# A fused convolution and gated MLP: one stream per row lane and bank, and a shorter fill

## Chip, cores, metric

One core of a Trainium2 chip. The metric is the device time of the program in microseconds (us), median of several runs. In profile lines PE is TensorE, PEld its weight loads, DVE VectorE, ACT ScalarE, POOL GpSimd, SPq and ACTq the queues on which SyncE and ScalarE issue transfers; L208 is line 208 of the kernel.

## Reference

```
x: (8, 4096, 192) f32; weight: (8, 7); w_in: (192, 2048); w_out: (2048, 192)
w   = softmax(weight, axis=-1)               # 8 heads of 24 channels, 7 taps
y   = causal convolution of x over tokens, w[head] for the head's 24 channels
h   = y.reshape(32768, 192) @ w_in
out = (h * cos(h)) @ w_out                   # f32
```

## The kernel before

Tokens run as two streams (batches 0 to 3 and 4 to 7), 512 tokens of each at a time: 32 such tiles, each with 16 *ups* and two *sets* of 16 *downs*, 64 sets in all.

- An **up** (U) makes 128 columns of `h` for both streams: six 64x512 matmuls in two row lanes of 64 rows. ScalarE then takes the cosine (S), VectorE multiplies (M).
- A **down** (d) adds two of these blocks into the output: eight 64x192 matmuls, again in two lanes. The lanes write different PSUM banks, and the program lets them trade banks only after a *mark*: a one-element memset on GpSimd that waits for the one lane's last matmul and is waited for by the next.
- A **convolution** (C and c, its halves) is done on TensorE with band matrices. Here the two lanes are the two halves of one 128-row window, so they add into the same banks and have to trade them once, with a mark:

```
def conv_first():
    ...
    end = lanes(half(0, 0, False), half(1, 1, False))
    return both, ps, (half(1, 0, True), half(0, 1, True)), end
...
elif op == "C":
    state["open"] = conv_first()
    state["mark"] = changeover(state["open"][3])
elif op == "c":
    conv_second(state["open"][2], state.pop("mark"))
```

- A convolved block is copied out of PSUM and transposed by a DMA (e). x is loaded in units, cast to bf16 by GpSimd (p), and loaded ahead.

```
nc.sync.dma_start(out=xw[:, s, :, :], in_=dram(x, base, [[D, 128], [W * D, NB], [1, D]]))   # 128 x 4 x 768 B
```

- The **fill** (k: the next weight load or cast) ends with the 16th up; then one order of operations is repeated for each set. Only what is emitted earlier on an engine or queue runs earlier there.

```
fill("kkkkUkSkMUSMUSMkUSMUSMCUScMekkkUSMkkUSMUSMCUScMekkkUSMkUSMkkkkUSMCUScMekkkkUSMUSMkU")
while count["y"] < 2 * NI:
    emit("dddSMdUdMSdUdMSdUMdSUdSMdUdSMCdcpdeMUdSdUyxUMS")
```

## Time and profile before

| | before |
|---|---|
| median of the 3 runs before the change was timed (range) | 741.77 us (741.24 to 743.03) |
| span of the profiled run | 739.7 us |
| first down | 46.87 us in the chain (46.70 in the timeline) |
| set with / without convolution | 11.02 / 10.46 us |
| end of the 62nd set to the end | 16.5 us |

Three stretches, to be read one by one: the start up to the first down, 62 sets bound by TensorE (50 with a convolution), and a tail. The prediction below shows the lines. Two more of the page will matter, from its parts on the DMA queues (packets, MB, share of 16 engines) and on the DMA issues (count, KB each, median us from issue to landing):

```profile
q1 hardware_dynamic: 126930, 69.88, 37.8%
...
xw<-in_x_dram SPq DMA_DIRECT2D x64, 384.0 KB, 5.4
```

This queue, with all loads of x and nearly all other traffic, stores too, keeps the DMA engines busy 37.8% of the span, and a 384 KB load of x lands 5.4 us after its issue (the median of 64).

### The profile page before, as it was taken

What the parts mean: (1) busy time and instruction counts of PE and PEld (TensorE: products, weight loads), DVE (VectorE), ACT (ScalarE), POOL (GpSimd) and SP (SyncE); (2) the same over time, 40 slices, a digit from 0 to 9 for tenths busy, and PEclk for the clock granted to TensorE, in tenths of its full rate; (3) what the DMA queues carried; (4) which work ended last, traced back from release to release, by engine and by line L of the source; (5) the groups of instructions that cost most, each with busy time, mean ns of one, the idle gap of its engine ahead of it and who ended that gap; (6) DMA issues with size and microseconds to landing.
All of it is one profiled execution on the core that took longest, in us unless ns stands there. A gap on an engine that the chain in (4) does not pass through costs nothing.

```text
span 739.7 us, 26852 instructions
## 1 busy us (share of the span) xinstructions
PE 707.4 (96%) x12044; PEld 518.1 (70%) x12044; DVE 644.3 (87%) x586; ACT 591.1 (80%) x642; POOL 86.1 (12%) x256
## 2 busy tenths in 40 slices
PE   1589999999999999999999999999999999999997
PEld 1257777777777777777777777777777777777776
DVE  1588998998989989989899899899899899999992
ACT  3588888888888888888888888888888887877871
POOL 2340110110110110110110110110111100000000
PEclk9999999999999999999999999999999999999999
DMA  8983453515344354342614615445332210111012
GB/s 188 290 207 70 107 125 77 137 50 155 70 121 112 68 128 116 105 122 70 156 39 110 160 43 144 98 104 140 74 95 61 70 53 25 44 45 44 24 45 66
DMA packets 127879, 73.17 MB, mean 99 GB/s; under 512 B 53907, under 2 KB 126099, under 8 KB 127764
## 3 DMA queue, kind: packets, MB, share of 16 engines
q1 hardware_dynamic: 126930, 69.88, 37.8%
q10 hardware_dynamic: 834, 1.57, 0.9%
q8 instruction: 94, 1.54, 0.9%
q14 instruction: 21, 0.17, 0.1%
HBM read 33.69 MB, written 25.17 MB: 80 GB/s over the span
## 4 chain that ended last, share of the span: by engine, by line
PE 93%; DVE 2%; DMA 2%; ACT 1%; issue 1%; SPq 0%; ACTq 0%; POOLq 0%; POOL 0%; DVEq 0%
PE h L208 48%; PE acc L208 45%; DVE g L332 2%; DMA cT<-ct 1%; ACT cos L327 1%; DMA row_d<-taps 1%; DMA turned<-row_d 0%; SPq L305 0%; ACT ct L297 0%; ACT L131 0%; PE h L404 0%; ACT osb L366 0%; DVE osb L366 0%; ACTq L78 0%; DVE band L159 0%
## 5 line engine op out<-in xcount | busy, mean ns | idle before, releaser
L332 DVE TENSOR_TENSOR g<-h,cos 128x1024 bf16<-128x1024 f32 x512 | 609.9, 1221 | 38.5 <-ACT cos L327 26.6
L327 ACT ACTIVATE cos<-h 128x1024 bf16<-128x1024 f32 x512 | 514.0, 1023 | 115.5 <-PE h L208 98.0
L208 PE MATMUL acc<-w,g 64*128 64x192 bf16 x8192 | 428.2, 243 | 1.3 <-ACT osb L366 0.8
L208 PEld LDWEIGHTS <-g 64*128 64x128 bf16 x8192 | 353.4, 94 | 101.8 <-POOL mark L218 1.4
L208 PE MATMUL h<-cT,w 64*128 64x512 bf16 x3072 | 408.8, 378 | 13.0 <-DMA cT<-ct 7.8
L208 PEld LDWEIGHTS <-w 64*128 64x128 bf16 x3072 | 148.7, 94 | 91.1 <-issue 18.5
L218 POOL MEMSET mark<- 1x1 f32 x117 | 10.3, 88 | 624.6 <-PE acc L208 447.9
L366 DVE COPY osb<-acc 128x384 f32<-128x384 f32 x64 | 35.7, 558 | 38.5 <-PE acc L208 38.4
L119 POOL CAST xb<-xw 128x512 bf16<-128x512 f32 x102 | 59.9, 616 | 6.5 <-DMA xw<-in_x_dram 5.3
L297 ACT CAST ct<-h 112x1024 bf16<-112x1024 f32 x51 | 51.6, 1012 | 10.5 <-PE h L208 9.0
L208 PE MATMUL h<-xb,band 64*128 64x192 bf16 (+5 forms) x760 | 41.7, 223 | 1.9 <-DVE g L332 1.9
L366 ACT COPY osb<-acc 128x384 f32<-128x384 f32 x64 | 30.3, 473 | 11.1 <-PE acc L208 11.1
L208 PEld LDWEIGHTS <-band 64*128 64x128 bf16 x760 | 25.8, 94 | 12.3 <-POOL mark L218 8.3
L404 PE MATMUL h<-xb,band 128*128 128x192 bf16 (+2 forms) x20 | 2.7, 330 | 12.0 <-DVE band L159 12.0
L404 PEld LDWEIGHTS <-band 128*128 128x128 bf16 x20 | 2.3, 143 | 12.1 <-DVE band L159 12.0
L175 POOL CAST w<-xw 128x512 bf16<-128x512 f32 x10 | 6.1, 641 | 9.7 <-DMA xw<-in_moe_w_in_dram 9.7
L159 DVE COPY band<-turned 128x512 bf16<-128x512 bf16 x1 | 0.3, 295 | 7.8 <-DMA turned<-row_d 7.8
L152 ACT CAST xb<-xw 128x768 bf16<-128x768 f32 x2 | 1.7, 831 | 4.0 <-DMA xw<-in_x_dram 4.0
L185 POOL CAST w<-xw 128x384 bf16<-128x384 f32 x8 | 3.7, 512 | 0.0
L175 DVE CAST w<-xw 128x512 bf16<-128x512 f32 x2 | 1.2, 630 | 2.4 <-DMA xw<-in_moe_w_in_dram 2.4
L294 ACT CAST ct<-h 112x512 bf16<-112x512 f32 x4 | 2.3, 585 | 0.9 <-PE h L208 0.9
L297 DVE CAST ct<-h 112x1024 bf16<-112x1024 f32 x1 | 1.2, 1224 | 2.0 <-PE h L404 2.0
(21 smaller groups left out, 15.2 us busy)
## 6 DMA issues: line engine op xcount, KB each, us to landing
xw<-in_x_dram SPq DMA_DIRECT2D x64, 384.0 KB, 5.4
out_dram<-osb SPq DMA_DIRECT2D x64, 384.0 KB, 3.2
xw<-in_x_dram SPq DMA_DIRECT2D x8, 336.0 KB, 4.9
xw<-in_moe_w_in_dram SPq DMA_DIRECT2D x4, 384.0 KB, 5.9
xw<-in_moe_w_in_dram ACTq DMA_DIRECT2D x4, 384.0 KB, 7.1
xw<-in_moe_w_out_dram SPq DMA_DIRECT2D x2, 768.0 KB, 12.1
cT<-ct SPq DMA_TRANSPOSE x67, 3.0
xw<-in_x_dram SPq DMA_DIRECT2D x8, 60.0 KB, 1.8
```

The source lines that it names most:

```text
L119: nc.gpsimd.tensor_copy(out=xb[:, :, :, ch], in_=xw[:, :, :, ch])
L152: copy(out=xb[:, s, :, :], in_=xw[:, s, :, :])
L175: copy(out=w1[:, q, c * CW:(c + 1) * CW], in_=staged[1, c][:, q, :])
L185: nc.gpsimd.tensor_copy(out=w2[:, c * n:(c + 1) * n, :][:, fs, :], in_=staged[2, c][:, fs, :])
L208: ins = nc.tensor.matmul(out=o, lhsT=w, rhs=r, start=start, stop=stop, skip_group_check=True)
L218: ins = nc.gpsimd.memset(mark, 0.0)
L294: nc.scalar.copy(ct[0:W, 0, :], ps[0:W, 0, :])
L297: copy(out=ct[0:W], in_=ps[0:W])
L327: nc.scalar.activation(out=cos, in_=hs[n], func=AF.Sin, bias=math.pi / 2.0, scale=1.0)
L332: nc.vector.tensor_tensor(out=g, in0=hs.pop(n), in1=cs.pop(n), op=ALU.mult)
L366: copy(out=osbs[k][:, 2 * bank:2 * bank + 2, :].rearrange("p a d -> p (a d)"), in_=acc[bank][:, 0:2 * D])
L404: nc.tensor.matmul(out=o, lhsT=band[:, h, :], rhs=r, start=True, stop=True)
```

## The change

Its intent: (1) a convolution on 64-row windows of 56 tokens, so that a lane is a *stream* and has a bank for itself, and no mark is needed; (2) downs in an order that works on the first 8 of 16 blocks longer, with three changes of bank in a set in place of one, so that the fill needs 13 ups in place of 16; (3) the first convolved blocks transposed by the idle array in place of DMA transposes, with 80 idle matmuls to keep its clock up, and loads spread on two queues; (4) the last set in an `h` tile of its own, woven between the downs of the set before, its store split on two queues.

```diff
-    W = 112
+    V = 56
+    BEFORE = L - V
+    W = 2 * V
... lane = (slice(0, L), slice(L, 128)): stream s uses partitions 64 s to 64 s + 63
-                nc.sync.dma_start(out=xw[:, s, :, :], in_=dram(x, base, [[D, 128], [W * D, NB], [1, D]]))
+            queue.dma_start(out=xw[lane[s], w0:w1, :], in_=dram(x, base + w0 * V * D, [[D, L], [V * D, w1 - w0], [1, D]]))
... convolution: lane l reads and writes stream l only
-        end = lanes(half(0, 0, False), half(1, 1, False))
+        mms = [conv_mms(p, ps, l) for l in range(2)]
+        half = len(mms[0]) // 2
+        lanes(*[m[:half] for m in mms])
... loads
-        nc.sync.dma_start(out=st, in_=moe_w_out[...])
+        nc.scalar.dma_start(out=st, in_=moe_w_out[...])
-    load_w1(0)
+    load_w1(0, (nc.scalar, nc.scalar))
     load_w1(1)                       # lower half on SyncE's queue, upper half on ScalarE's
+    load_ahead(1, (nc.sync, nc.scalar))
... turns of the downs
+    TURNS = ((0, 0), (0, 1), (1, 0), (1, 1), (1, 2), (0, 2), (0, 3), (1, 3))
-        if j == 7:
-            state["turn"] = changeover(end)
+        if j < 15 and TURNS[(j + 1) // 2][0] != flip:
+            turns[k] = changeover(end)
... start
+    for _ in range(80):
+        nc.tensor.matmul(out=idle[0:W, 0, 0:W], lhsT=one, rhs=one, start=True, stop=True)
+    ... two convolutions, 15 transposes as matmuls against an identity, four copies
-    fill("kkkkUkSkMUSMUSMkUSMUSMCUScMekkkUSMkkUSMUSMCUScMekkkUSMkUSMkkkkUSMCUScMekkkkUSMUSMkU")
-    while count["y"] < 2 * NI:
-        emit("dddSMdUdMSdUdMSdUMdSUdSMdUdSMCdcpdeMUdSdUyxUMS")
+    fill("kkkkUSMkUSMkUSMkkkkUSMkUSMCcUSMekkCcUSMekkkUSMCcUSMekkkkkkkkUSMUSMUSMkU")
+    for k in range(NSETS - 2):
+        emit("dddSMdUdMSUdSdMUdSMdU" + ("CcpdMSeU" if k == 1 else "dMSU") + "dSdMCcdedMUdpSdUyxUMS")
+    last = h_pool.tile([128, 2, T], FP32, name="h")
+    emit("dddMSdUdMSUdSdMUdSMdMM" + "tttt" + "dddddtttttt" + "ddxytttttt" + "xy")      # t: downs of the last set
```

## The prediction

> **What bounds the kernel now.** I read the busy times first, then the chain of work that ended last in three windows, then the list of waits, then the moved bytes in stretches of 2 us.
>
> ```profile
> PE 707.4 (96%) x12044; PEld 518.1 (70%) x12044; DVE 644.3 (87%) x586; ACT 591.1 (80%) x642; POOL 86.1 (12%) x256
> ...
> PE   1589999999999999999999999999999999999997
> ...
> PE 93%; DVE 2%; DMA 2%; ACT 1%; issue 1%; SPq 0%; ACTq 0%; POOLq 0%; POOL 0%; DVEq 0%
> ```
>
> TensorE is the bound from the third of the 40 slices to the last, and the chain is 93% TensorE. So there are three separate places to gain: the start, the middle, the tail. The start, from the chain between 0 and 60 us:
>
> ```profile
> 3.84 4.35 DMA row_d<-taps
> 8.27 3.34 DMA turned<-row_d
> ...
> 17.05 6.50 DMA cT<-ct
> ...
> 23.59 3.18 PE h L208 x14
> ...
> 46.87 1.32 PE acc L208 x32
> ```
>
> Columns are start, length, what. Two DMA round trips build the band matrices, three transposing DMAs turn the first convolved blocks, the first up-projection ("up") really starts at 23.59, the first output product ("down") at 46.87. Between the last two TensorE is fed by VectorE and ScalarE one tile at a time. The middle, the same view between 300 and 312 us, at the convolution:
>
> ```profile
> 306.74 0.65 PE h L208 x6
> 307.39 0.33 PE acc L208 x8
> 307.72 0.22 PE h L208 x8
> 307.94 0.33 PE acc L208 x8
> 308.27 0.34 PE h L208 x8
> 308.61 0.33 PE acc L208 x8
> ```
>
> An up is 0.65 us, a down 0.33. The convolution's two halves have equal columns, yet the second takes 0.34 and the first 0.22: it waits for the one-element GpSimd mark that tells that the lanes may change banks. A set (8 ups, 16 downs) takes 11.02 us with a convolution and 10.46 without (starts of successive long downs in the chain, 46.87 to 57.89 and 598.14 to 608.60). The waits give the matching line:
>
> ```profile
> PEld L208 <- POOL mark L218: 9.7, 53, 0.5
> ```
>
> 53 waits, one for each convolution; the 64 down marks leave no such stall but in the tail, since an up lies between the two turns: down, up, down at 304.45 to 305.43 is as quick there as elsewhere. The tail, in the chain:
>
> ```profile
> 722.67 0.48 ACT osb L366
> 723.15 0.04 issue
> 723.20 2.83 PE acc L208 x64
> ...
> 732.80 2.86 PE acc L208 x64
> 735.66 0.55 DVE osb L366
> ```
>
> The last two sets have only downs left, done one set after the other, with two bare marks and a bare emptying of the banks between: 723.20 to 735.66 = 12.46 us for 32 downs (32 x 0.328 = 10.5), then the copy and the store to 739.7.
>
> **What the Trainium skill says.** (1) "TensorEngine Tiling (Array Packing)", Gotcha 1: different row tiles must not use one PSUM bank at once. That is why the lanes need marks, and why a bank for each lane needs none. (2) "TensorE: Matmul & The Clock Gate", Wait — 56ns, not 53.3ns?: a warm matmul costs N/2.4 + about 2.5 ns. The trace agrees: 128 of 192 columns and 48 of 512 in two lanes are 10.24 us plus 88 x 2.5 ns = 10.46, the measured set. So the middle has nothing more to give but the convolution. (3) The same page, What's actually happening: the array runs at half clock until some 3.4 us of activity. The trace agrees: the 20 matmuls of the first ups took 4.09 us at 23.59, later six took 0.65 us. (4) "DMA: Bandwidth & Descriptors", Anatomy of one DMA: about 2 us are fixed in each transfer. Here even the 0.2 KB load of the taps landed 1.24 us after issue, and the 2.2 KB row took 4.35 us behind 1.57 MB of x, so most of the latter is queueing.
>
> **The change, part by part.**
>
> *Convolution.* Each lane takes one stream and one bank; two 64-row windows of 56 tokens replace one 128-row window in two halves. Matmuls per usual tile (12 or 16) and columns (1024 per lane) stay. The mark goes. New cost: 1024/2.4 GHz = 0.427, plus 6 to 8 per lane x 2.5 ns = 0.445 us, against 0.555. The loop has 62 sets: before 62 x 10.46 + 50 x 0.555 = 676.3 (measured, 46.87 to 723.20: 676.3); after, 51 of the 56 convolutions fall into it (2 + 3 come earlier): 62 x 10.46 + 51 x 0.445 = **671.2 us, -5.1**. Loads, casts (616 ns), evacuations (1012 ns) and transposes keep their size.
>
> *Turns of the output product.* Three changes of bank in a set in place of one, 192 down marks for 64. In the order of operations each has an up of 0.65 us between; a mark's way is about 0.35 us (0.27 idle in the tail plus the drain), so I count 0. The order lets the first downs use the first 8 f tiles, so the fill needs 13 ups in place of 16. Marks can be late only behind GpSimd casts (2 x 0.62 us), which are placed over 2 us before the next one.
>
> *Start.* Taps ready at 3.8 as before. The row goes on the other queue and behind 0.98 MB of x, which at the 239 to 267 GB/s of the first 8 us has landed by some 6.2: row at 6.1 (estimate). Two half-size turned loads issue to 6.8 and land at about 9.5 beside the w1 loads, band copy 0.3: **convolution at 9.9**, against 11.99. The 80 idle matmuls of 112 columns start at about 2.6 and end by 9 to 10 (31 cold ones of 107 ns, the rest 56 to 80), so the clock is up. Two tiles 0.9 us, evacuation 1.0 to 1.2, transposes by the array 15 x 0.06 to 0.1, four copies in pairs of 0.6 each, handovers: about 3.8 us, so **first up at 13.7**, against 23.59. Before, the fill from first up to first down was 23.3 us = 16 x 1.22 (the multiply, 1221 ns) + 3 convolutions x 1.27. For 13 ups: 15.9 + 3.8 = 19.7, plus 0.6 for two more DMA issues on ScalarE's queue: 20.3. **First down at 34.0.** But the marks of the first set stand behind all weight and x casts on GpSimd. They need 8.8 MB; at 250 GB/s for x alone and 320 (seen 28 to 36 us) for the mix, with three transposes, this has landed at 33 to 34, and the last casts end at 35 to 37, where the first turn wants its mark at 36. I charge 1.2 us: **loop starts, in effect, at 35.2**.
>
> *Tail.* Three ups are left as well, and the last set, in its own h tile, is woven between the downs of the one before: 32 x 0.328 + 3 x 0.65 = 12.5, two bare marks 0.5, copy and drain 0.7, store in two halves on two queues 2.8: **16.5 us**, against 16.5 before without the three ups. So this part earns 2 us, spent on the shorter fill.
>
> *Sum.* 35.2 + 671.2 + 16.5 = 722.9 us span, against 739.7: -16.8. The timed runs are 2.1 us above the span: **725.0 us**, a gain of 2.3%. The same by causes: 11.7 earlier at the loop, of which 3 ups and a convolution (2.5) are done later; 5.1 from the convolution; 2.5 back from the tail.
>
> **Rivals.**
> 1. *The transfers decide the start.* The fill is 10 us earlier but needs nearly the same bytes. For: before, the DMA share was above 1 from 12 to 38 us, and the x load for the last cast of the fill landed at 44.8. Against: three transposes of 6.5 us are gone from it, and the up fill itself is slower than the loads. If loads run at 250 GB/s throughout, the first turn waits to about 40: 729 us, within 2%.
> 2. *The added marks cost after all.* 128 more; at 0.05 us each, 6.4 us, and the gain of the convolution is gone: 731 us. Against: the 64 old ones cost nothing measurable.
> 3. *VectorE becomes the bound.* It works 8 x 1.221 + 0.558 = 10.33 us a set; a set without convolution has 10.46, one with it now 10.91. With three h tiles I find 0.1 to 0.3 us slack at each up; if those are used up in the 51 convolution sets at 0.1 us each, 730 us. For it: the multiplies now come later in the order; against: 10.33 is still below 10.46.
> 4. *The start is better than I think*: turned at 8, fill not held back: 31 to 32, 721 us.
>
> **Range and chances.** The middle is sure to about 1.5 us, start to 3, tail to 1. Low is rival 4 with luck, high is rival 1 plus a part of 2: 719.5 to 731. The 2% border is 726.9, only 1.9 us above my time, so chances follow from that: faster 0.66, same 0.33, slower 0.01.
>
> **What would show it.** In the changed profile: the convolution at 9 to 11, first up at 13 to 15 and first down at 32 to 36; a mid-run convolution set of 10.9 us with no waits for marks in it, and 10.46 without; the list of waits without TensorE waiting for marks beyond some 2 us in all; from the end of the 62nd set 16 to 17 us. Wrong would be: first turn of the first set later than 38 with GpSimd waiting for x or w loads (rival 1), sets of 11 us with TensorE waiting for marks (2) or for the multiply (3), or a band that comes after 11.

## The result

738.4 us (737.64 to 740.11, 4 runs) against 741.62 (4 runs) before: a ratio of **0.9956** with a 95% interval of 0.9934 to 0.9979, so the same within 2%, and outside the predicted range. Ratios here are the mean time of one kernel's runs over that of the other's runs of the same rounds, so not quite the ratio of the medians quoted. The unaltered changed kernel was run again later: 738.62 us, 0.9948.

The span fell from 739.7 to 738.3 us (the profiled run was the slowest of its four). The page of the changed kernel:

```profile
PE 712.4 (96%) x12271; PEld 565.9 (77%) x12271; DVE 640.4 (87%) x590; ACT 588.8 (80%) x637; POOL 94.0 (13%) x340
...
PEclk7689999999999999999999999999999999999999
...
q1 hardware_dynamic: 121712, 66.42, 42.7%
...
PE 93%; DMA 4%; issue 1%; DVE 1%; ACT 1%; POOL 1%; ACTq 0%; SPq 0%; POOLq 0%; DVEq 0%
...
xw<-in_x_dram SPq DMA_DIRECT2D x60, 384.0 KB, 8.0
```

The chain has 4% of DMA where it had 2%. The queue moves *less* (66.42 for 69.88 MB; 3 MB of weights went to the other queue) and is busy *longer* (42.7 for 37.8%); a load of x lands after 8.0 us, not 5.4. The array's granted clock is below full in the first slices.

**The middle is as predicted.** The chain between 309 and 321 us (start, length, what), a set with a convolution:

```profile
309.65 1.32 PE acc L254 x32
...
316.83 0.46 PE h L254 x10
...
320.55 0.49 PE acc L254 x12
```

The convolution is one piece of 0.46 us (0.445 predicted) with no wait for a mark, and the set takes 320.55 - 309.65 = 10.90 us (10.905 predicted). The list of waits between 55 and 720 us:

```profile
PEld L254 <- POOL mark L264: 0.8, 2, 0.4
```

Two waits of 0.4 us for about 190 marks (before, in the same window: 50 waits, 8.6 us). So the added marks cost 0.8 us at most there.

**The start is not.** The chain between 0 and 60 us:

```profile
3.85 4.02 DMA row_d<-taps
...
8.48 7.76 DMA turned<-row_d
...
20.82 2.76 PE h L254 x12
...
23.67 16.43 DMA xw<-in_moe_w_out_dram
...
40.15 1.86 POOL w L219 x4
...
47.01 1.11 POOL xb L156 x2
48.12 0.04 POOL mark L264
```

The band's data ("turned") takes 7.76 us, 16.24 us instead of 9.5; the first up runs at 20.82, not 13.7. Then the chain is a load: w2 on its way for 16.4 us, its casts, the cast of x behind it, and then the mark for the first turn. GpSimd's operations between 8 and 56 us (start, length, what, and in brackets the idle time before with its cause) show what came late before that:

```profile
29.19 0.61 POOL L156 CAST xb<-xw 128x512 bf16<-128x512 f32 x1 [8.25 <-DMA xw<-in_x_dram]
32.03 1.73 POOL L209 CAST w<-xw 128x512 bf16<-128x512 f32 x3 [2.23 <-DMA xw<-in_moe_w_in_dram]
```

The second half of blocks 5 to 12 landed at 29.2 us, and the first convolution of the fill waited for it (3.10 us). The second waited 3.81 us more, but not for x: its casts stood on GpSimd behind the cast of w1, whose load came at 32.0. The first down came at 45.88 us, 0.8 us earlier than before (46.70 in the same view), where 34 was predicted. The DMA engines were busy all the time: the first 35 us moved, by the busy times in stretches of 5 us, (111 + 218 + 205 + 198 + 207 + 278 + 227) x 5 us = 7.2 MB, against 8.2 MB in the kernel before. Two of those stretches, each with the busy time of five engines, the granted clock, the DMA share and GB/s:

```profile
15.00:20.00 5.00, 3.04 (x79) 2.56 (x80) 1.60 (x3) 1.20 (x2) 1.73 (x3) 0.50 1.12 198
20.00:25.00 5.00, 4.85 (x29) 2.31 (x29) 2.50 (x4) 3.06 (x5) 0.61 (x1) 0.55 1.11 207
```

A full DMA share (1.12; a packet is counted where it starts, so a share can pass 1) at 198 GB/s; in the kernel before the stretches at a full share between 10 and 45 us had 206 to 328 GB/s.

**The tail** is 1.3 us longer than predicted. The operations between 726 and 740 us:

```profile
727.63 1.49 PE L254 MATMUL acc<-w,g 64*128 64x192 bf16 x32 [0.58 <-POOL mark L264]
...
734.23 0.48 ACT L398 COPY osb<-h 128x384 f32<-128x384 f32 x1 [1.92 <-PE h L254]
...
734.74 0.56 DVE L398 COPY osb<-h 128x384 f32<-128x384 f32 x1 [2.39 <-ACT osb L398]
```

The two bare marks took 0.58 and 0.27 us, 0.85 together where 0.5 was predicted, and the two last copies ran one after the other (VectorE names ScalarE's copy as its releaser). From the last long run of downs of the loop (720.49) to the end it took 17.8 us, three ups included.

### The profile page after: what moved, and what is told of

The parts are those of the page before. It is cut to its first block, busy times and chain, and to the rows that moved or that the text cites. A ratio compares the mean times of both kernels' runs of the same rounds, so it can differ in the third digit from the quotient of the medians.

```text
span 738.3 us, 27466 instructions
## 1 busy us (share of the span) xinstructions
PE 712.4 (96%) x12271; PEld 565.9 (77%) x12271; DVE 640.4 (87%) x590; ACT 588.8 (80%) x637; POOL 94.0 (13%) x340
## 3 DMA queue, kind: packets, MB, share of 16 engines
q1 hardware_dynamic: 121712, 66.42, 42.7%
## 4 chain that ended last, share of the span: by engine, by line
PE 93%; DMA 4%; issue 1%; DVE 1%; ACT 1%; POOL 1%; ACTq 0%; SPq 0%; POOLq 0%; DVEq 0%
PE h L254 48%; PE acc L254 45%; DMA xw<-in_moe_w_out_dram 2%; DMA turned<-row_d 1%; DMA row_d<-taps 1%; DVE g L361 0%; POOL w L219 0%; ACT L170 0%; POOL xb L156 0%; ACT cos L356 0%; ACT ct L309 0%; PE acc L456 0%; DVE osb L398 0%; ACTq L79 0%; ACT cT L459 0%
## 5 line engine op out<-in xcount | busy, mean ns | idle before, releaser
L254 PEld LDWEIGHTS <-g 64*128 64x128 bf16 x8192 | 374.8, 94 | 84.2 <-POOL mark L264 2.8
L254 PE MATMUL h<-cT,w 64*128 64x512 bf16 x3072 | 423.7, 380 | 1.7 <-DVE g L361 1.6
L254 PEld LDWEIGHTS <-w 64*128 64x128 bf16 x3072 | 179.0, 95 | 63.2 <-issue 7.8
L264 POOL MEMSET mark<- 1x1 f32 x192 | 16.9, 88 | 608.1 <-PE acc L254 599.5
L309 ACT CAST ct<-h 112x1024 bf16<-112x1024 f32 (+1 forms) x55 | 55.3, 1006 | 14.6 <-PE h L254 10.7
L156 POOL CAST xb<-xw 128x512 bf16<-128x512 f32 (+1 forms) x110 | 64.4, 615 | 14.9 <-DMA xw<-in_x_dram 14.0
L254 PE MATMUL h<-xb,band 64*128 64x192 bf16 (+8 forms) x912 | 38.0, 218 | 15.6 <-DVE band L237 7.8
L254 PEld LDWEIGHTS <-band 64*128 64x128 bf16 x912 | 32.8, 96 | 17.7 <-DVE band L237 8.0
L443 PE MATMUL h<-one 128*112 128x112 bf16 x80 | 6.6, 274 | 2.2 <-POOL one L186 2.2
L443 PEld LDWEIGHTS <-one 128*112 128x112 bf16 x80 | 6.5, 188 | 2.2 <-POOL one L186 2.2
## 6 DMA issues: line engine op xcount, KB each, us to landing
xw<-in_moe_w_out_dram ACTq DMA_DIRECT2D x2, 768.0 KB, 20.3
```

The costliest lines, as they stand in the source:

```text
L156: copies[j % len(copies)](out=xbs[p][:, s0:s1], in_=src)
L254: ins = nc.tensor.matmul(out=o, lhsT=w, rhs=r, start=start, stop=stop, skip_group_check=True)
L264: ins = nc.gpsimd.memset(mark, 0.0)
L309: copy(out=ct[0:W, 0:n].rearrange("p j s c -> p s j c"), in_=ps[0:W, :, 0:n * L].rearrange("p s (j c) -> p s j c", c=L))
L443: nc.tensor.matmul(out=idle[0:W, 0, 0:W], lhsT=one, rhs=one, start=True, stop=True)
```

## The experiments

Three theories of why the start gained 1 us and not 12, as the expectations name them. **A**: the late band. **B**: the bytes that have to land before the first downs and turns, and their order. **C**: the loads of x became slow, because they span 64 partitions. Ratios are to the kernel before in the same rounds; "third set" is the start of the third set's long run of downs, the place from which all versions of the changed kernel are alike: from there to the end of the span it is 667.8 to 669.4 us in each with the new tail, 670.3 in e4 without it, and 671.0 to 671.2 in the kernel before, e3a and e3b. (In e8 and e9 the ups are done in another order, so it has no counterpart.)

| run | median us | ratio (95%) | first down | third set |
|---|---|---|---|---|
| the kernel before | 741.62 | 1 | 46.70 | 68.75 |
| the change | 738.40 | 0.9956 (0.9934-0.9979) | 45.88 | 68.95 |
| the change again | 738.62 | 0.9948 (0.9933-0.9963) | 44.62 | 67.34 |
| e1 turned first | 742.29 | 1.0006 (0.9991-1.0021) | 49.79 | 72.50 |
| e2 w2 before x | 737.94 | 0.9944 (0.9924-0.9965) | 44.63 | 67.34 |
| e3a before, 64-partition loads | 751.66 | 1.0130 (1.0113-1.0147) | 54.60 | 78.01 |
| e3b before, half loads | 742.86 | 1.0009 (0.9994-1.0024) | 47.76 | 69.81 |
| e4 tail undone | 739.32 | 0.9962 (0.9947-0.9977) | 44.18 | 67.11 |
| e5 order of need | 736.76 | 0.9925 (0.9908-0.9941) | 43.63 | 66.90 |
| e6 no idle matmuls | 737.44 | 0.9928 (0.9909-0.9947) | 44.92 | 67.63 |
| e7 128-partition loads (wrong) | 735.93 | 0.9918 (0.9898-0.9937) | 43.97 | 66.81 |
| e8 convolutions after the ups | 741.81 | 0.9994 (0.9977-1.0011) | 32.20 | - |
| e9 the same, 128 (wrong) | 738.23 | 0.9944 (0.9922-0.9966) | 32.45 | - |
| e10 x before the last of w1 | 737.23 | 0.9924 (0.9911-0.9938) | 35.71 | 67.51 |
| e11 later x after transposes | 737.54 | 0.9946 (0.9933-0.9960) | 34.94 | 66.85 |
| e12 the same, 128 (wrong) | 732.63 | 0.9877 (0.9864-0.9891) | 34.25 | 63.57 |
| **e13 cast behind the marks** | **730.96** | **0.9864** (0.9849-0.9879) | 35.64 | 60.69 |
| e14 halves on two queues | 733.65 | 0.9885 (0.9870-0.9901) | 39.59 | 63.52 |
| e15 as e13, 128 (wrong) | 728.38 | 0.9820 (0.9806-0.9833) | 35.22 | 59.15 |

"Wrong" marks results that are wrong: the loads have the right size and shape, but lanes get the wrong rows. All others are correct.

**The unaltered kernel again**, for its spread beside e8 to e10:

> The changed kernel unaltered, to have it beside the next two on one chip and to see how much its start varies: 737 to 740, first down between 43 and 46.

738.62 us. Its start was 1.3 us better than in the first profile, so differences below that between starts are not read. Its band was there at 14.5 us and its first up at 18.95, against 16.4 and 20.82 in the first profile.

### e1: the band first (theory A)

```diff
-    load_w1(0, (nc.scalar, nc.scalar))
-    load_w1(1)
-    load_ahead(1, (nc.sync, nc.scalar))
+    load_w1(0, (nc.sync, nc.sync))
+    load_w1(1, (nc.sync, nc.sync))
+    load_ahead(1)
```

> The changed kernel with the first w1 chunks and the next x blocks issued on SyncE's queue, which puts them behind the two loads of the turned taps; only the row of taps stays on ScalarE's queue. Theory A (the late band costs the start, because 1.2 MB of w1 and more were put ahead of the turned taps): turned lands at about 11.5 us in place of 16.2, the first up at about 16 in place of 20.8, first down at 41 to 42 in place of 45.9, time 734 (-4 us). Theory B (the start is bound by the sum of bytes that must land before the first downs, w2 last): band and first up come earlier as in A, but w2 still lands at 45 or later, first down at 45 to 47, time within 1.5 us of the changed kernel's 738.4.

The band was there at 11.8 us (its copy ended then) and the first up at 16.5, so the late band *was* queueing. Yet the time grew by 4 us: with all loads behind the band on one queue, 97 to 108 GB/s were moved in the first 10 us, x landed at 25.9 and 33.1 us, and the first convolution of the fill stood 10.86 us for it. **A alone falls**: the run put other loads later to have the band first, and what was not moved early was missed later.

### e2: w2 before later x (theory B, one link)

```diff
-        nc.scalar.dma_start(out=st, in_=moe_w_out[...])
+        nc.sync.dma_start(out=st, in_=moe_w_out[...])
... and the cast of blocks 13 to 20 moved behind the first turn
```

> The changed kernel with w2 loaded on SyncE's queue ahead of blocks 13 to 20 of x, and with the cast of those blocks moved from the fill to behind the first turn of the first set; the band is as late as before. Theory B (bytes before the first down): 1.57 MB less stand before the first down, at the 250 GB/s seen between 20 and 40 us that is 6 us, so w2 lands at about 39, first down at 40 to 42, time 732 to 734. Theory A: the band at 16.4 and the cold clock set the fill, first down stays at 44 to 46, time 737 to 739.

GpSimd cast w2 at 36.39 us without a wait, so the link that the chain named was gone. Yet the time, 737.94 us, was that of the unaltered kernel and not the 732 to 734 of theory B (third set at 67.34 us in both). The chain's last link was not the only one: the wait for x in the fill was right behind it.

### e3a and e3b: how loads are cut (theory C)

In the kernel *before*, each load of x cut in two, by partitions or, as a control, by blocks:

```diff
-                nc.sync.dma_start(out=xw[:, s, :, :], in_=dram(x, base, [[D, 128], [W * D, NB], [1, D]]))
e3a:
+                    nc.sync.dma_start(out=xw[l * 64:l * 64 + 64, s, :, :], in_=dram(x, base, [[D, 64], [W * D, NB], [1, D]]))
e3b:
+                    nc.sync.dma_start(out=xw[:, s, 2 * l:2 * l + 2, :], in_=dram(x, base, [[D, 128], [W * D, 2], [1, D]]))
```

> The kernel before with each regular x load cut in two loads of 64 partitions (same bytes, twice the loads). Theory C (loads into 64 partitions move fewer bytes a second, which is why the changed kernel's x packets of 768 B take 52 ns where the old ones take 42): DMA share of the whole span rises from 38% to about 42%, the x loads of the start land later, first down at 48 to 50 in place of 46.9, time +1 to +3 us. Rival: packets are slower in the changed kernel only for the two queues at once and the order of loads: share and time stay, within 0.5 us.

> Control for the run with 64 partitions: each regular x load of the kernel before cut in two loads of all 128 partitions and half the blocks (same bytes, same number of loads as there). Theory C expects DMA share and time as in the kernel before, 741 to 742 us. If this one moves as much as the 64-partition one, it is the number of loads and not the partitions.

Same bytes, rows and number of loads; 751.66 against 742.86 us. The pages of the two, first e3a:

```profile
q1 hardware_dynamic: 127954, 69.89, 43.7%
...
xw<-in_x_dram SPq DMA_DIRECT2D x128, 192.0 KB, 5.2
```

then e3b:

```profile
q1 hardware_dynamic: 127954, 69.89, 38.2%
...
xw<-in_x_dram SPq DMA_DIRECT2D x128, 192.0 KB, 4.5
```

Over all packets of the queue, stores too, a packet costs 0.437 x 16 x 749.2 / 127954 = 40.9 ns of an engine on 64 partitions and 0.382 x 16 x 741.0 / 127954 = 35.4 ns on 128 (the two spans are 749.2 and 741.0 us). The first down moves from 47.76 to 54.60 us. **C is shown**, with 8.8 us in the kernel before, nearly all in the start (8.2 us at the third set); in the middle slower loads cost next to nothing.

### e7: the changed kernel with 128-partition loads

```diff
+            if w1 - w0 == 2 * n:
+                queue.dma_start(out=xw[:, s * n:(s + 1) * n, :], in_=dram(x, base, [[D, 128], [V * D, n], [1, D]]))
+            else:
                 queue.dma_start(out=xw[lane[s], w0:w1, :], in_=...)
```

> The changed kernel with each x load of its two streams made over all 128 partitions and half the windows: same bytes, same number of loads, same 768 B packets, wrong data on purpose (results are wrong). Theory C (64-partition loads are what slows the start): rate in the start rises from 200 to 225 GB/s to 250 to 300, DMA share of the span falls from 43% to 38 or 39%, x for blocks 5 to 12 lands by 24 in place of 29.2, w2 by 36 to 40, first down at 38 to 41, time 731 to 734. If the order of the loads alone is to blame, share may fall but first down stays at 45 to 46 and the time at 737 to 738.

The queue's share fell to 35.5% and x landed by 26.4 us, but the time was 735.93: 0.3 to 0.4% of gain (0.9918 against 0.9956 and 0.9948), 2 to 3 us and not the 4 to 7 expected, and the first down came at 43.97, not 38 to 41. C is a cause in the changed kernel too, but a small part of the 13 us missing.

### e5: loads in the order of need, convolutions later

```diff
+    load_w1(1, (nc.sync, nc.sync))
+    load_w1(2, (nc.sync, nc.sync))
+    load_w1(3, (nc.sync, nc.sync))
     load_ahead(1)
... w2 on SyncE's queue, ahead of blocks 13 to 20; casts in the same order
-    fill("kkkkUSMkUSMkUSMkkkkUSMkUSMCcUSMekkCcUSMekkkUSMCcUSMekkkkkkkkUSMUSMUSMkU")
+    fill("k" * 23 + "USM" * 9 + "CcUSMe" * 3 + "U")
```

> The changed kernel with its loads in order of need (first w1 chunk on ScalarE's queue as now, then on SyncE's queue turned taps, the other three w1 chunks, blocks 5 to 12 of x, w2, blocks 13 to 20), the three convolutions of the fill moved behind the ninth up, and the cast of blocks 13 to 20 moved behind the first turn. Theory B, sharpened by the last runs (after w2 was put first, the fill still waited until 28.4 us for x of blocks 5 to 12, which its first convolution needs after five ups): ups 1 to 9 run from 18 to 30 while x lands, first down at 37 to 41, time 731 to 734. If the fill is bound by its own chain of ScalarE, VectorE and a cold array, first down stays at 43 or later and time above 735.

Nine ups were done by 27.6 us, the last five of them 1.13 us apart, and then TensorE waited (timeline, 22 to 46 us):

```profile
33.31 1.04 PE L256 MATMUL h<-xb,band 64*128 64x192 bf16 x12 [5.66 <-POOL xb L156]
```

The wait only moved. First down and time (43.63 and 736.76 us) are those of the rival in the expectation, but what this line names is a wait for x, not the fill's own chain.

### e4 and e6: the tail, and the idle matmuls

```diff
e4:
-    emit("dddMSdUdMSUdSdMUdSMdMM" + "tttt" + "dddddtttttt" + "ddxytttttt" + "xy")
+    emit("dddMSdUdMSUdSdMUdSMdMM" + "dddddddxy" + "tttttttttttttttt" + "xy")      # last set in acc, as before
e6:
-    for _ in range(80):
+    for _ in range(1):
```

> The changed kernel with the last set in the ordinary output banks, after the set before it, as in the kernel before; three turns in each set. I claimed 2 us for this part: from the last long run of downs (720.5) to the end 19.5 to 20.5 in place of 17.8, time 740 to 741. If the marks and serial copies of the new tail eat it, within 0.7 us of 738.

> The changed kernel with one idle matmul in place of 80. The band came at 16.4, 7.6 us after the idle ones ended, and the convolutions of the start ran at half clock anyway, so I expect no effect: time within 0.7 us of the changed kernel, the first up within 0.3 us of 20.8.

e4: from the last long run of the loop to the end 737.4 - 717.36 = 20.0 us against 17.8, so the woven tail earns 2.2 us, as predicted (2). Its start happened to be 1.8 us faster, so its time (739.32) missed the 740 to 741 expected; read this from the traces and not from the times. e6: 0.9928, no slower than with the 80 matmuls (0.9956, 0.9948). Its first up came at 18.93, outside the 0.3 us around 20.8 that were expected, but as in the unaltered kernel run again (18.95). In the changed kernel they end at 8.9 us, TensorE then waits 7.85 us for the band, and the clock is down again: 0.50 granted between 15 and 20 us (above).

### e8 and e9: the first downs without waiting for the convolutions

```diff
-    fill("kkkkUSMkUSMkUSMkkkkUSMkUSMCcUSMekkCcUSMekkkUSMCcUSMekkkkkkkkUSMUSMUSMkU")
+    fill("k" * 23 + "USM" * 12 + "U")
+    emit("dddSMdUdMSUdSdMUdSMd" + "dMCceddCceddCcedppd" + "yx")
... (second set with three convolutions between ups and downs); e9: with the loads of e7
```

> The load order of the run before (w1, then w2, then x of blocks 5 to 12), but with no convolution in the fill: 13 ups of the first tile, then the first downs, the three convolutions between the downs of the first set, and three more with 13 ups in the second set. Theory B sharpened (the fill's convolutions wait for x that only the 17th up needs): the ups run without a stop, first down at 33 to 36 in place of 43.6 to 45.9; the second set is paced by VectorE (16 tiles of 1.22) so part is given back; the third set starts at 63 to 66 in place of 69.1, time 732.5 to 735. Rival (the fill is slow by itself: half clock, ScalarE issuing loads): first down not before 40, time above 736.

> The last run with x loads over 128 partitions (wrong data on purpose). If partitions and order are two separate causes, another 1 to 2 us faster than that run; if with the convolutions out of the fill the transfers are no longer on the path, within 1 us of it.

The first down came at 32.20 us, but the gain was lost, and more. TensorE's timeline of e8:

```profile
41.08 0.82 PE L255 MATMUL acc<-w,g 64*128 64x192 bf16 x8 [6.73 <-POOL mark L265]
```

Four downs later the first turn stood 6.73 us for its mark: on GpSimd the mark (40.93 us) came right behind casts of x, whose loads had landed at 34.3 and 38.2. The time, 741.81 us, missed the 732.5 to 735 expected. e9 is 3.6 us faster than e8, more than the 1 to 2 expected; its wait is 3.37 us. So the partitions cost in this order too, and are a cause beside the order.

### e10, e11, e13: one link after the other

e10 loads x before the last quarter of w1, and puts late casts behind the first mark:

```diff
+    load_w1(1, (nc.sync, nc.sync))
+    load_w1(2, (nc.sync, nc.sync))
     load_ahead(1)
+    load_w1(3, (nc.sync, nc.sync))
... w2 on SyncE's queue; casts in the order of the loads
+    fill("k" * 19 + "USM" * 9 + "CceUSM" * 3 + "U")
-        emit("dddSMdUdMSU..." )
+        fill("dddSMdUd" + ("kkkkp" if k == 0 else "") + "MSU...")
```

> Correct version meant to beat both: loads in the order w1 first three quarters, x of blocks 5 to 12, last quarter of w1, w2, blocks 13 to 20; the three convolutions of the fill after the ninth up, each emptied by ScalarE ahead of the next cosine (with the other order each cost 3.5 us in the run with loads in order of need); the casts of the second half of w2 and of blocks 13 to 20 stand on GpSimd behind the first turn's mark, because the run without convolutions in the fill showed that mark waiting 6.7 us behind casts. Theory B sharpened: x lands by 29, each convolution costs some 2 us of the fill, first down at 36.5 to 39, third set at 60 to 63 in place of 67.5 to 69.1, time 731 to 733.5. If the fill holds the start for another reason, first down stays at 43 and the time at 736 or more.

The first down came at 35.71 us, and then the 17th up, the first to need blocks from the fill's convolutions:

```profile
46.68 2.05 PE L256 MATMUL h<-cT,w 64*128 64x512 bf16 x6 [5.88 <-DMA cT<-ct]
```

Its transposes were issued at 36.24 us, behind x loads that SyncE had been issuing from 26.45 to 36.1 us. e11 moves those loads behind the transposes, and e12 adds the loads of e7:

```diff
-        yield lambda: load_ahead(1)
         yield from (lambda q=q: cast_w2(0, q) for q in range(4))
+        yield lambda: load_ahead(1)
         yield from (lambda q=q: cast_w2(1, q) for q in range(4))
-    fill("k" * 19 + "USM" * 9 + "CceUSM" * 3 + "U")
+    fill("k" * 18 + "USM" * 9 + "CceUSM" * 3 + "kU")
```

> The version with x loads before the last quarter of w1, with one thing moved: the loads of blocks 13 to 20 are issued after the three transposes of the fill instead of before them. There the seventeenth up waited 5.88 us for the transposed values and the third set started at 67.69 us. If the order of issue held it (the transposes were issued at 36.24 us, after the x loads had been issued from 26.45 to 36.1 us), the transposes now go out about when the convolutions are evacuated, near 33 us, the seventeenth up runs without that wait, the third set starts at 62 to 65 us and the time is 732 to 735 us. If the bytes of the x loads hold it, the wait only moves to blocks 13 to 20, the third set stays at 67 to 68 us and the time at 736 to 738 us.

> The same with x loads over 128 partitions (wrong result on purpose: the lanes get the wrong rows). If the order of issue was the last link, this gains the 2 to 3.6 us that the wider loads brought in two other pairs of runs, to 729 to 733 us; if nothing but bytes holds the third set, it is within 1 us of the other.

e11 missed in time: 737.54 us. But the 17th up ran at 40.83 without a wait; the stall was again at the next thing in line. TensorE's timeline of e11:

```profile
40.83 0.83 PE L256 MATMUL h<-cT,w 64*128 64x512 bf16 x6
48.86 1.46 PE L256 MATMUL acc<-w,g 64*128 64x192 bf16 x16 [7.20 <-POOL mark L266]
```

and GpSimd's:

```profile
48.16 0.61 POOL L156 CAST xb<-xw 128x512 bf16<-128x512 f32 x1 [2.49 <-DMA xw<-in_x_dram]
48.71 0.09 POOL L266 MEMSET mark<- 1x1 f32 x1
```

A mark of the first set stood behind casts of x (the first waited 6.66 us for its load) that only this set's one convolution needs, and that convolution can be done a set later. e12, with wider loads, was 4.9 us faster, its wait 4.18.

e13 moves that cast behind the set's last mark, and the set's one convolution into the next:

```diff
-        fill("dddSMdUd" + ("kkkkp" if k == 0 else "") + "MSUdSdMUdSMdU" + ("CcpdMSeU" if k == 1 else "dMSU") + "dSdMCcdedMUdpSdUyxUMS")
+        fill("dddSMdUd" + {0: "kkkk", 1: "Ccpe"}.get(k, "") + "MSUdSdMUdSMdU" + ("CcpdMSeU" if k == 1 else "dMSU")
+             + ("dSdMddMUdpSdUyxUMS" if k == 0 else "dSdMCcdedMUdpSdUyxUMS"))
```

> As the version with x loads after the transposes, with the cast of blocks 13 to 20 behind the last mark of the first set and that set's one convolution moved into the second set, which then has three. If the cast's place on GpSimd held the start, the first set runs without the 7.20 us wait and its neighbours, from about 35 to 46.5 us, the second set with its three convolutions takes 12 to 14 us (values of x land at 45 to 48 us, at most 3 us of wait), the third set starts at 59 to 62 us instead of 67 to 68, and the time is 729 to 733 us. If the bytes hold it, the wait moves to the convolutions of the second set, which then starts its successor at 66 us or later, and the time stays above 735 us.

**730.96 us, 0.9864, correct**: within the expectation, 6.6 us faster than e11 and the best correct version. TensorE's timeline of e13 (the second line is the end of the first set and the start of the next):

```profile
35.64 1.50 PE L256 MATMUL acc<-w,g 64*128 64x192 bf16 x32
...
46.10 1.50 PE L256 MATMUL acc<-w,g 64*128 64x192 bf16 x32
...
49.18 0.51 PE L256 MATMUL acc<-w,g 64*128 64x192 bf16 x8 [0.94 <-POOL mark L266]
...
60.69 1.50 PE L256 MATMUL acc<-w,g 64*128 64x192 bf16 x32
```

The first set takes 46.10 - 35.64 = 10.46 us, the undisturbed time; the second, with three convolutions, 14.6. The loads were no faster than in e11 (204 and 213 GB/s between 20 and 30 us, against 207 and 214). So those 6.6 us were order alone (two moves, of which the convolution's follows from the cast's): **a mark queued behind a cast that waits for a load.**

### e14 and e15: the 64 partitions once more

e14 puts lower and upper halves of w1 and of blocks 5 to 12 on two queues, to have both halves under way at once; e15 is e13 with the loads of e7.

```diff
e14:
-    load_w1(1, (nc.sync, nc.sync))
+    load_w1(1)                                # SyncE's queue and ScalarE's
... the same for the other two quarters of w1
-    load_ahead(1)
+    load_ahead(1, (nc.sync, nc.scalar))
```

> The version with the cast behind the marks, with the loads of the second to fourth quarter of w1 and of blocks 5 to 12 issued on two queues, lower 64 partitions on SyncE's and upper 64 on ScalarE's, so that both halves are under way at once. The Trainium skill, SBUF - State Buffer, section Door 1: The DMA port swizzle, says that partitions 0 to 63 reach only half of the ports (196 GB/s measured there against 328 for all 128). If that is the cause and two queues mix the halves, the rate between 10 and 30 us rises from 204 to 226 GB/s to 260 or more, the last x of blocks 5 to 12 lands at 23 to 25 us instead of 28.3, and the time falls by 2 to 4 us to 727 to 729 us. If the two halves take turns all the same, or the number of rows is the cause, the rate stays below 235 GB/s and the time within 1 us of 731.

> The version with the cast behind the marks, with x loads over 128 partitions (wrong result on purpose, the lanes get wrong rows). In two other pairs this brought 3.6 and 4.9 us. If the start of that version is now held by x landing at 28.3 and 48.4 us (0.94 us of wait for the mark behind the second), wider loads bring 1 to 4 us: 727 to 730 us, with the wait for the mark gone. If the fill and VectorE hold it, it stays within 1 us of 731.

e14 met neither expectation: 211 and 201 GB/s between 10 and 20 us (e13: 226 and 218), but 260 and 258 between 20 and 30 (e13: 204 and 213), where w2, over 128 partitions, had been issued too. It was 2.7 us slower (1.6 by the ratios; the two ran in different rounds), because two x loads held ScalarE's queue from 14.39 to 18.80 us, and the copy behind them let TensorE wait 3.83 us. Whether ports are the mechanism stays open. e15 took 728.38 us, as expected, with the wait for the mark gone and the fill paced by VectorE's multiplies: 64-partition loads still cost e13 2.6 us (3.3 by the ratios). Between 20 and 30 us e15 moved 291 and 230 GB/s, e13 204 and 213.

## Why the prediction was wrong

The predicted span was 35.2 + 671.2 + 16.5 = 722.9 us; measured were 45.88 + 674.6 + 17.8 = 738.3. The 15.4 us missing are 10.7 in the start, 3.4 in the loop and 1.3 in the tail. (45.88 is read in the timeline; the chain counts a first down 0.17 us later, as in the kernel before, so 0.2 of the 3.4 belong to the start.)

- **Convolution: right** (10.90 for 10.905 us a set, no waits for marks). Rivals 2 and 3 are out: waits for marks came to 0.8 us between 55 and 720 us, and the set without a convolution still takes 10.46 us. The bank rule of point (1) was not tested: no run lets two lanes into one bank without a mark. For point (3) it is the doubled durations that agree; the granted clock in the trace of before reads 1.00 even there.
- **Start: the step that failed.** The prediction let the loads land in time and charged only 1.2 us for waiting. Its first terms were "row at 6.1" and turned loads that "land at about 9.5": they landed at 7.87 and 16.24, behind loads of x and w1 (turned at 11.5 in e1, where only the first x loads were ahead of them). Its last was "at 250 GB/s for x alone and 320 (seen 28 to 36 us) for the mix ... this has landed at 33 to 34": measured were 198 to 218 GB/s between 5 and 25 us at a full DMA share, and w2 landed at 45.15 us. Of the 11.9 us by which the first down was late (45.88 for 34.0), 7.1 stood before the first up (20.82 for 13.7) and 4.8 in the fill. The runs give the sizes: a better order of loads, convolutions and casts alone, with loads on 64 partitions, brought 738.4 to 730.96 us (e13); loads on 128 partitions alone 735.93 (e7); both 728.38 (e15); 725.0 was predicted. So order is the larger part and the rate the smaller.
- **Rate.** The predicted rates were read off the kernel before, whose x loads span 112 or 128 partitions; the change makes them 64. e3a against e3b shows what that costs. The Trainium skill has it in "SBUF — State Buffer", Door 1: The DMA port swizzle: partitions 0 to 63 reach only half of the ports, 196 GB/s measured there against 328 for all 128. This agrees in size: 200 to 214 GB/s between 20 and 30 us in e10, e11 and e13, against 230 to 301 in e12 and e15, which differ from e11 and e13 in the x loads alone. The prediction did not draw on that page: it said of the loads that they keep their size, which is true, and missed that their shape changed. The trace of before held a hint too: 223 GB/s between 10 and 15 us at a DMA share of 1.02, where its first w1 loads, which span 64 partitions each, were under way.
- **A link behind the late band**: from 8.31 to 16.86 us ScalarE's queue was held by the issue of two x loads (8.55 us), so ScalarE could not have copied out the first convolution before, even with the band at 9.5. e1 moved these loads together with the band, so the two are not told apart.
- **Rival 1**, the transfers decide the start, was the right one and mis-sized: 729 us was put on it, with the first turn at 40; the mark came at 48.07.
- **The fill**: "13 ups: 15.9" assumed a warm array and a fill that is not held back. It took 25.1 us from the first up to the first down, where 20.3 was predicted: it waited 3.10 us for x and 3.81 us for casts of x, and was cold after the second wait (12 matmuls of ups took 2.63 us, 1.46 when warm). In e13 and e15 the first down came at 35.64 and 35.22 us, near the 34.0 predicted, but partly by luck: the first up came late (17.15 and 18.16, not 13.7), and the fill took 18.5 and 17.1 us, less than the 20.3 predicted.
- **Order**, which the prediction saw ("the marks of the first set stand behind all weight and x casts on GpSimd") and charged with 1.2 us, is worth 6.6 us by itself once the fill is fast (e13 against e11). In the change as it is, it was hidden behind the slower fill. That e1, e2, e5, e10 and e11 each removed one wait and gained little or nothing fits this.
- **Loop**, 3.4 us more than predicted. From the starts of the sets' first downs in the timeline: the first set took 11.28 us, 0.4 over a set with a convolution, with the first turn's late mark in it; the second took 11.80, but it has two convolutions, so it is 0.45 over 10.46 + 2 x 0.445, with VectorE and ScalarE in its chain; nine later sets are 2.5 us over together, 1.45 of it in the two that start at 429.40 and 495.85 us, where the profile names only issue. None of these was tested by a run.
- **Tail**: 2 us of gain right (2.2 by e4); the 1.3 us missed are 0.35 on bare marks (0.85 for 0.5), 0.6 on drain and copies (1.3 for 0.7, as one copy ran after the other), 0.2 on the store (3.0 for 2.8) and 0.2 in the downs. Why the second copy waits for the first was not tested.

The 1.4 us of the profiled pair are therefore 0.8 from the start (46.70 to 45.88, both in the timeline), 1.9 from the loop (676.5 to 674.6) and -1.3 from the tail, where three ups more are done (16.5 to 17.8).

## What to carry to other kernels

A change that cuts a tile differently can keep its bytes and lose load rate: look at how many partitions each load spans before taking a GB/s figure from the old trace. A start can be, as here, a chain of several waits with nearly the same end, so that removing the one that the profile names shows little until the last of them falls; follow the wait from one version to the next, as from e10 to e13. And on an engine that works in order, as GpSimd does in the timelines of e8 and e11, put short marks that the bound engine waits for ahead of work that waits for loads.

## What the Trainium skill lacked or had wrong

- "TensorEngine Tiling (Array Packing)", Gotcha 1, names the banks of row tiles, but not that a lane of 64 rows tends to bring loads on 64 partitions. Here these cost 8.8 us in the kernel before (e3a against e3b: DMA share 43.7 against 38.2%) and 2.6 us in the best version (e15 against e13).
- "SBUF — State Buffer", Door 1, is not wrong: its 196 GB/s for 64 partitions is near what a stream of mostly such loads got here (198 to 218 GB/s). "DMA: Bandwidth & Descriptors", Rules for kernel authors, says that two transfers to disjoint halves serialize. e14 had 201 to 211 GB/s between 10 and 20 us with w1 and x on two queues, which agrees, and 258 to 260 between 20 and 30 us with w2 among them, which leaves it open.
- "DMA: Bandwidth & Descriptors", Anatomy, has for DMAs issued from GpSimd a fixed part and a part in bytes, and no page has a term for what is queued ahead: here, issued from SyncE, the turned loads (2 x 64 KB) took 7.76 us behind other loads and 5.07 us in e15. Nor does a page give a figure for how long issuing holds an engine when much is under way: two issues held ScalarE's queue 8.55 us in the changed kernel and 4.41 us in e14.
